# Laying out a whole kernel's instructions by due times, with shared buffers and PSUM banks

## The chip, the cores and the metric

One core of a Trainium2 chip runs the kernel. The metric is the device time of one execution in microseconds, as a median over runs. The kernel before takes 353.24 us (three runs, 352.86 to 353.85). Runs carry a state, fast or slow; unless said otherwise every number below comes from fast runs.

## The reference

A polysketch attention (4 batches, 4 heads, sequence 1088, head size 32, sketch size 8), whose output of 128 columns goes through a phase mixing over the tokens:

```python
def phi(x):
    a = np.einsum('rd,bhsd->bhsr', S1, x)
    b = np.einsum('rd,bhsd->bhsr', S2, x)
    return np.einsum('bhsi,bhsj->bhsij', a, b).reshape(*x.shape[:-1], r * r)
q_p, k_p = phi(q), phi(k)
kv  = np.einsum('bhsf,bhsd->bhfd', k_p, v)
num = np.einsum('bhsf,bhfd->bhsd', q_p, kv)
den = np.einsum('bhsf,bhf->bhs', q_p, np.sum(k_p, axis=2))[..., None] + 1e-06
x = num / den                                # (B, S, 128) after the heads are joined
theta = x @ w_theta
yr = np.einsum('ts,bsd->btd', w_tok_r, x * np.cos(theta))
yi = np.einsum('ts,bsd->btd', w_tok_i, x * np.sin(theta))
u = x + yr + yi
out = u + np.maximum(u @ w_ch, 0.0)
```

The two `w_tok` matrices (1088 x 1088) arrive as 64-bit floats and are turned into fp32 on the chip, in 34 pieces of 128 x 544. Each piece costs one load, three ScalarE instructions and two VectorE instructions (the tiles `st`, `step`, `wT`). PSUM is the memory into which TensorE puts its results, in eight banks that the kernel gives out. In names of tiles: `z` are the inputs of the mixing (they lie in two of the staging buffers, so the profile calls them `zst` before and `st` after the change), `lv` the feature levels of the queries, `fl`, `dn` and `rd` the denominators, `feat` the products of features, `uT` and `ot` the output, `cm` and `tl` small matrices made from the keys; `cut_r` and `cut_z` belong to many short steps that split small matrices into fp16 levels.

## The kernel before

It uses fixed pools and a fixed order of five priority levels, in which weight conversion goes along with batch 0's attention:

```python
ps_w = ctx.enter_context(tc.tile_pool(name="ps_w", bufs=3, space=PSUM))
ps_acc = ctx.enter_context(tc.tile_pool(name="ps_acc", bufs=2, space=PSUM))
ps_y = ctx.enter_context(tc.tile_pool(name="ps_y", bufs=3, space=PSUM))
# ... cut
levels = {nm: state.cur_priority + i * 100000
          for i, nm in enumerate(("first", "weights", "out", "attention", "mixing"))}
# ... cut
def load_f32(dst, src):               # one weight piece
    # ... cut
    st = stg.tile([P, PIECE], I64, tag="st", name="st")[:p, :n]
    nc.sync.dma_start(st, src)
    lo, hi = split(st)
    step = stg.tile([P, PIECE, 2], I16, tag="step", name="step", bufs=2)[:p, :n]
    x = dst.bitcast(I32)
    A.activation(dst, hi.bitcast(F32), AF.Copy, scale=2.0**-112)
    A.activation(step[:, :, 1].bitcast(F16), hi.bitcast(F32), AF.Copy, scale=2.0**-60)
    A.activation(step[:, :, 0], lo.bitcast(U32), AF.Copy, scale=2.0**-29)
    ts(x, x, 3, ALU.logical_shift_left)
    tt(V, x, x, step.rearrange("p n t -> p (n t)").bitcast(I32), ALU.add)
# ... cut
    matrices(0); keys_values(0, spare); attention(0)      # level "first"
with level("attention"):
    keys(1)
    attention(1)
    keys(2)
mixing(0, True)
with level("attention"):
    attention(2)
    keys(3)
mixing(1, False)
# ... batches 2 and 3 alike
```

Of the kernel before, what the change touches and what calls it, by code (L numbers as in the profile page):

```python
# [38 lines left out]
TINY = 2.0**-60  # L39
PIECE = 544  # L40


@with_exitstack
def kernel(
# [23 lines left out]
    const = ctx.enter_context(tc.tile_pool(name="const", bufs=1))  # L68
    stg = ctx.enter_context(tc.tile_pool(name="stg", bufs=4))
    ld = ctx.enter_context(tc.tile_pool(name="ld", bufs=1))  # L70
    work = ctx.enter_context(tc.tile_pool(name="work", bufs=2))
    sm = ctx.enter_context(tc.tile_pool(name="sm", bufs=2))
    xp = ctx.enter_context(tc.tile_pool(name="xp", bufs=2))
    ps_w = ctx.enter_context(tc.tile_pool(name="ps_w", bufs=3, space=PSUM))
    ps_acc = ctx.enter_context(tc.tile_pool(name="ps_acc", bufs=2, space=PSUM))
    ps_y = ctx.enter_context(tc.tile_pool(name="ps_y", bufs=3, space=PSUM))

    V, A = nc.vector, nc.scalar



    state = tc.trace_state
    levels = {nm: state.cur_priority + i * 100000
              for i, nm in enumerate(("first", "weights", "out", "attention", "mixing"))}

    @contextmanager
    def level(nm):
        kept, state.cur_priority = state.cur_priority, levels[nm]
        yield
        levels[nm], state.cur_priority = state.cur_priority, kept  # L90
# [10 lines left out]

    def psum(pool, tag, dt=F32, n=512):
        return pool.tile([P, n], dt, tag=tag, name=tag)
# [14 lines left out]
    def load_f32(dst, src):  # L118






        p, n = dst.shape
        if src.dtype == F32:
            nc.sync.dma_start(dst, src)
            return
        st = stg.tile([P, PIECE], I64, tag="st", name="st")[:p, :n]
        nc.sync.dma_start(st, src)  # L130
        lo, hi = split(st)
        step = stg.tile([P, PIECE, 2], I16, tag="step", name="step", bufs=2)[:p, :n]
        x = dst.bitcast(I32)
        A.activation(dst, hi.bitcast(F32), AF.Copy, scale=2.0**-112)  # L134
        A.activation(step[:, :, 1].bitcast(F16), hi.bitcast(F32), AF.Copy, scale=2.0**-60)  # L135
        A.activation(step[:, :, 0], lo.bitcast(U32), AF.Copy, scale=2.0**-29)  # L136
        ts(x, x, 3, ALU.logical_shift_left)
        tt(V, x, x, step.rearrange("p n t -> p (n t)").bitcast(I32), ALU.add)

    def load_pair(src, n, tag, copies=1):  # L140

        p = src.shape[0]
        m = p * copies
        hi = const.tile([P, n], F32, tag=f"{tag}_hi", name=f"{tag}_hi")[:m]
        lo = const.tile([P, n], F32, tag=f"{tag}_lo", name=f"{tag}_lo")[:m]
        if src.dtype == F32:
            for i in range(copies):
                nc.sync.dma_start(hi[i * p:(i + 1) * p], src)
            V.memset(lo, 0.0)
            return hi, lo  # L150
        st = const.tile([P, n], I64, tag=f"{tag}_st", name=f"{tag}_st")[:m]
        for i in range(copies):
            nc.scalar.dma_start(st[i * p:(i + 1) * p], src)
        wl, wh = split(st)
        x = magnitude(hi, wh)
        y = const.tile([P, n], I32, tag=f"{tag}_y", name=f"{tag}_y")[:m]
# [4 lines left out]
        z = const.tile([P, n], I32, tag=f"{tag}_z", name=f"{tag}_z")[:m]  # L161
# [6 lines left out]
    ident = const.tile([P, P], F32, tag="ident", name="ident")  # L168
    make_identity(nc, ident)
    ones = const.tile([P, P], F32, tag="ones", name="ones")  # L170
    V.memset(ones, 1.0)
    halfpi = const.tile([P, 1], F32, tag="halfpi", name="halfpi")
    V.memset(halfpi, math.pi / 2.0)

    hm = const.tile([P, H], F32, tag="hm", name="hm")
# [3 lines left out]
    hmT = const.tile([P, P], F32, tag="hmT", name="hmT")[:H]  # L179
    t_ = psum(ps_acc, "acc")  # L180
    nc.tensor.transpose(t_[:H, :P], hm, ident)
    A.activation(hmT, t_[:H, :P], AF.Copy, scale=512.0)

    bdm = const.tile([P, H, D], F32, tag="bdm", name="bdm")
    ts(bdm, hm.unsqueeze(2).to_broadcast([P, H, D]), 2.0**-15, ALU.mult)

    hmf = const.tile([P, 6, H], F32, tag="hmf", name="hmf")
# [9 lines left out]
    def powers(m, n, lhs=None, pool=(ps_acc, "acc")):  # L197


        t = psum(*pool)  # L200
        nc.tensor.transpose(t[:n, :P], m, ident)
        mx = sm.tile([P, 1], F32, tag="mx", name="mx")[:n]
# [4 lines left out]
        dg = sm.tile([P, H], F32, tag="dg", name="dg")[:n, :n]  # L207
        ts(dg, ident[:n, :n], mx, ALU.mult)
        o = psum(*pool)
        nc.tensor.matmul(o[:, :n], ones[:n, :], dg, start=True, stop=lhs is None, skip_group_check=True)  # L210
        w = n
        if lhs is not None:
            nc.tensor.matmul(o[:, w:w + 1], lhs, mx, start=False, stop=True, skip_group_check=True)
            w += 1
        s = sm.tile([P, H + 1], F32, tag="pw", name="pw")
# [3 lines left out]
    def cut4(dst, x0, rest, c0, c1, near=1, p=P):  # L219
# [3 lines left out]
        r = sm.tile([P, (B - 1) * P], F32, tag="cut_r", name="cut_r", bufs=1)[:p, :n]  # L223
        z = sm.tile([P, (B - 1) * P], F32, tag="cut_z", name="cut_z", bufs=1)[:p, :n]
# [19 lines left out]
    def spread(m, cs, z):  # L244

        o = m[:, :, cs].rearrange("p l (h r) -> p l h r", h=H)
        for o_, z_, f in ((o[:, 0:4], z, hmf[:, 0:4]), (o[:, 4:6], z[:, 0:2], hmf[:, 4:6])):
# [7 lines left out]
    def load(b, names):  # L255
        for nm in names:
            src = {"k": k, "q": q, "v": v}[nm]
            t = ld.tile([P, NC, H, D], F32, tag=f"ld_{nm}", name=f"ld_{nm}")
            nc.sync.dma_start(t.rearrange("p c h d -> p (c h d)"), src[b].rearrange("p c h d -> p (c h d)"))
            tiles[nm, b] = t  # L260

    ipk = const.tile([P, B, 2, H], F32, tag="ipk", name="ipk")
    gm = const.tile([P, 2, B, H], F32, tag="gm", name="gm")
    kvbd = []
    for b in range(B):
        t = const.tile([P, 2, 2 * D], F32, tag=f"kvbd{b}", name=f"kvbd{b}")
# [3 lines left out]
    w2 = const.tile([P, 2, DM], F32, tag="w2", name="w2")  # L270
    wT = const.tile([P, NK, S], F32, tag="wT", name="wT")


    def keys_slices(b):

        kn = tiles["k", b]
        m4 = sm.tile([P, H], F32, tag="m4", name="m4")
# [5 lines left out]
        kx = work.tile([P, NC, H, D], F32, tag="qx", name="kx", bufs=1)  # L283
# [3 lines left out]
        ks = work.tile([P, 3, NC * P], F16, tag="ksl", name="ksl", bufs=1)  # L287
# [7 lines left out]
    def keys_sums(b, cm, pool=(ps_acc, "acc")):  # L295
# [3 lines left out]
        gp = psum(*pool).rearrange("p (x n) -> p x n", x=4)  # L299

        for c in range(NC):
            cs = slice(c * P, (c + 1) * P)
            nc.tensor.matmul(gp[:, 0:3], ks[:, 1, cs], ks[:, 0:3, cs],
                             start=(c == 0), stop=False, skip_group_check=True)
            nc.tensor.matmul(gp[:, 0:4:3], ks[:, 2, cs], ks[:, 0:3:2, cs],
# [3 lines left out]
        t = psum(ps_acc, "acc")[:, :2 * P].rearrange("p (x n) -> p x n", x=2)  # L309
        for i in range(2):  # L310
            nc.tensor.transpose(t[:, i], cm[:, 2 * i], ident)
        tt(V, cm[:, 0:3:2], cm[:, 0:3:2], t, ALU.add)

    def keys_matrix(bs, cm):
# [3 lines left out]
        cz = work.tile([P, NL, nb, P], F16, tag="cz", name="cz", bufs=1)  # L318
# [3 lines left out]
        tp = psum(ps_acc, "acc")[:, :nb * NL * R].rearrange("p (b l r) -> p b l r", b=nb, l=NL)  # L322
        for i in range(nb):
            for l in range(NL):
                nc.tensor.matmul(tp[:, i, l:NL], cz[:, l, i], sz[:, 0:NL - l, 0:R],
                                 start=(i == 0 and l == 0), stop=(l == NL - 1), skip_group_check=True)
        n = nb * R
        tl = sm.tile([P, NL, nb, R], F32, tag="tl", name="tl", bufs=1)
        V.tensor_copy(tl.rearrange("p l b r -> p b l r"), tp)
        tl = tl.rearrange("p l b r -> p l (b r)")  # L330
        tz = sm.tile([P, NL, n], F16, tag="tz", name="tz", bufs=1)
# [406 lines left out]
```

## Time and profile before

| | before |
|---|---|
| span of the profiled run | 354.1 us |
| TensorE, VectorE, ScalarE busy | 271.9, 237.8, 167.0 us |
| first input of batch 0's mixing (z) | 117.45 us |
| TensorE idle (span less busy) | 82.2 us |

In the profile, PE is TensorE, PEld its weight loads, DVE VectorE, ACT ScalarE, POOL GpSimd and SP the load queue. One more view is needed for the comparison later: the windows of the profile, cut at 91, 120 and 165 us. The columns are window, length, busy time of PE, PEld, DVE, ACT and POOL with their instructions, granted clock, DMA share and GB/s.

```profile
0.00:91.00 91.00, 33.56 (x157) 24.63 (x157) 69.26 (x265) 70.93 (x124) 0.70 (x6) 0.76 0.68 229
91.00:120.00 29.00, 13.72 (x48) 10.20 (x49) 24.51 (x41) 19.46 (x34) 0.00 (x0) 0.50 0.20 69
120.00:165.00 45.00, 44.83 (x248) 31.60 (x247) 28.98 (x93) 17.05 (x39) 0.00 (x0) 0.97 0.13 40
165.00:350.00 185.00, 179.54 (x904) 124.83 (x902) 115.08 (x284) 59.06 (x136) 0.00 (x0) 0.98 0.07 22
```

At 165 us 179.8 us of TensorE's work is still to come (0.2 us of it after 350 us, where the window ends), and the span ends 9.3 us later than 165 + 179.8. A busy TensorE runs at nearly full clock there (0.98), so the time left is the work left. In the first 120 us TensorE was busy for 47.3 us, much of it at half clock.

### The profile page before, as it was taken

Reading aid. Unit: us, or ns where it says so; the run is one execution under the profiler, and the core shown is the slowest. Engines: PE = TensorE matmul, PEld = TensorE weight load, DVE = VectorE, ACT = ScalarE, POOL = GpSimd, SP = SyncE. Lnnn points to the kernel's source line nnn. Section 1 sums busy time; section 2 is a strip of 40 time slices with the busy share of each in tenths; the row PEclk is TensorE's granted clock in tenths of the full one; section 3 lists DMA queues with packets and bytes.
Section 4 is the critical chain, followed back from the end, with each engine's and each line's share of the span. In section 5 each row is a group of like instructions: output and inputs, shape, how many; then the busy total and the mean of one; then the engine's idle time right before and its main releaser. Section 6 shows DMA issues by size and latency. Waiting matters only on the chain.

```text
span 354.1 us, 4014 instructions
## 1 busy us (share of the span) xinstructions
PE 271.9 (77%) x1355; PEld 191.3 (54%) x1355; DVE 237.8 (67%) x681; ACT 167.0 (47%) x333; POOL 0.7 (0%) x6
## 2 busy tenths in 40 slices
PE   0406680127236799999978999999999999999994
PEld 0304480014125576675646778567776866776662
DVE  4897868884998178748986576887769289332111
ACT  0799839999955556043113365132456320442000
POOL 0000000000000000000000000000000000000000
PEclk9999955556555599999987999999999999999998
DMA  7668519884800004010010014000000000000000
GB/s 276 228 236 280 168 62 311 274 297 149 274 22 1 2 1 136 0 67 1 2 44 19 2 67 129 6 23 24 1 19 2 0 24 0 23 20 0 22 22 19
DMA packets 11604, 28.78 MB, mean 81 GB/s; under 512 B 1216, under 2 KB 5568, under 8 KB 11584
## 3 DMA queue, kind: packets, MB, share of 16 engines
q1 hardware_dynamic: 11376, 28.51, 24.1%
q8 instruction: 10, 0.16, 0.2%
q14 instruction: 10, 0.08, 0.1%
q10 hardware_dynamic: 208, 0.02, 0.0%
HBM read 26.30 MB, written 2.23 MB: 81 GB/s over the span
## 4 chain that ended last, share of the span: by engine, by line
PE 62%; DVE 17%; ACT 13%; DMA 4%; issue 1%; ACTq 0%; SPq 0%
PE y L560 31%; PE w L513 5%; ACT step L135 3%; PE acc L395 3%; ACT step L136 3%; PE w L533 3%; PE y L395 2%; PE w L507 2%; ACT lv L447 2%; PE y L570 2%; DVE wT L93 2%; PE w L385 2%; DMA s_t_st<-s_t 2%; ACT wT L134 2%; DVE kx L93 1%
## 5 line engine op out<-in xcount | busy, mean ns | idle before, releaser
L560 PE MATMUL y<-wT,zst 128*128 128x384 f32 (+1 forms) x384 | 134.9, 482 | 2.0 <-DVE zst L93 1.9
L560 PEld LDWEIGHTS y<-wT,zst 128*128 128x128 f32 x384 | 68.7, 193 | 32.2 <-DVE zst L93 3.2
L579 ACT COPY ot<-y 128x384 f32<-128x384 f32 (+2 forms) x16 | 5.9, 398 | 58.3 <-PE y L574 53.9
L135 ACT ACTIVATE step<-st 128x544 f16<-128x544 f32 (+1 forms) x35 | 27.8, 794 | 6.0 <-DVE wT L93 6.0
L513 PEld LDWEIGHTS w<-kvbd,qpT 128*128 128x128 f32 x144 | 22.0, 217 | 13.0 <-ACT qpT L511 11.0
L136 ACT ACTIVATE step<-st 128x544 int16<-128x544 uint32 (+1 forms) x35 | 27.5, 786 | 0.0
L93 DVE CUSTOM_DVE_ANT_0 wT<-wT,step 128x1088 uint16<-128x1088 uint16 x34 | 24.4, 718 | 4.5 <-ACT step L136 3.8
L513 PE MATMUL w<-kvbd,qpT 128*128 128x64 f32 x144 | 24.4, 305 | 3.8 <-ACT qpT L511 3.7
L134 ACT ACTIVATE wT<-st 128x544 f32<-128x544 f32 x34 | 23.2, 685 | 2.0 <-DMA st<-w_tok 1.9
L93 DVE TENSOR_TENSOR uT<-xT,y 128x384 f32<-128x384 f32 (+1 forms) x12 | 6.3, 528 | 22.5 <-PE y L560 22.5
L511 ACT COPY qpT<-w 128x256 f32<-128x256 f32 x36 | 12.7, 368 | 18.0 <-PE w L507 17.5
L507 PE MATMUL w<-ident,qp 128*128 128x128 f32 x72 | 14.0, 299 | 7.9 <-DVE qp L93 7.9
L530 ACT COPY xT<-w 128x384 f32<-128x384 f32 x12 | 5.7, 476 | 25.2 <-PE w L528 25.2
L100 DVE SCALAR_TENSOR_TENSOR tt<-tn,w 128x384 f32<-128x384 f32 x12 | 6.6, 552 | 14.9 <-ACT tn L537 14.9
L447 ACT COPY lv<-w 128x384 f32<-128x384 f32 x36 | 14.9, 499 | 2.9 <-PE w L446 2.9
L97 DVE TENSOR_SCALAR wT<-wT 128x544 int32<-128x544 int32 x34 | 14.6, 434 | 1.7 <-ACT wT L134 1.6
L507 PEld LDWEIGHTS w<-ident,qp 128*128 128x128 f32 x72 | 9.9, 168 | 8.9 <-ACT wT L134 7.9
L93 DVE TENSOR_TENSOR kp<-ks 128x768 f32<-128x768 f32 x12 | 11.4, 953 | 4.5 <-PE acc L395 2.5
L444 PE MATMUL w<-mv,q 128*128 128x384 f16 x36 | 13.2, 368 | 0.9 <-DVE mv L93 0.9
L395 PEld LDWEIGHTS acc<-ld_v,kp 128*128 128x128 f32 x108 | 13.1, 192 | 1.5
L93 DVE TENSOR_TENSOR zst<-x,tn 128x384 f32<-128x384 f32 (+1 forms) x12 | 6.1, 512 | 11.3 <-ACT tn L540 11.3
L533 PEld LDWEIGHTS w<-w,xT 128*128 128x128 f32 x72 | 10.7, 215 | 5.0 <-ACT xT L530 4.4
(228 smaller groups left out, 503.8 us busy)
## 6 DMA issues: line engine op xcount, KB each, us to landing
st<-w_tok SPq DMA_DIRECT2D x34, 544.0 KB, 4.6
ld_k<-k_l SPq DMA_DIRECT2D x4, 576.0 KB, 4.0
ld_q<-q_l SPq DMA_DIRECT2D x4, 576.0 KB, 4.3
ld_v<-v_l SPq DMA_DIRECT2D x4, 576.0 KB, 3.6
out<-ot SPq DMA_DIRECT2D x8, 192.0 KB, 2.1
out<-ot SPq DMA_DIRECT2D x4, 128.0 KB, 1.8
st<-w_sq SPq DMA_DIRECT2D x1, 256.0 KB, 4.5
out<-ot SPq DMA_DIRECT2D x4, 32.0 KB, 1.9
```

Source lines behind the costliest of these rows:

```text
L93: eng.tensor_tensor(out=o, in0=a, in1=b, op=op)
L97: V.tensor_scalar(out=o, in0=a, scalar1=s1, scalar2=s2, op0=op0, **kw)
L134: A.activation(dst, hi.bitcast(F32), AF.Copy, scale=2.0**-112)
L135: A.activation(step[:, :, 1].bitcast(F16), hi.bitcast(F32), AF.Copy, scale=2.0**-60)
L136: A.activation(step[:, :, 0], lo.bitcast(U32), AF.Copy, scale=2.0**-29)
L395: nc.tensor.matmul(kv[:, n], kp[:, i * H + 2 * n:i * H + 2 * n + 2].rearrange("p h i j -> p (h i j)"), vn[:, c, 2 * n:2 * n + 2].rearrange ...
L444: nc.tensor.matmul(lp, q0, flat[:, 0:4 * W], start=True, stop=False, skip_group_check=True)
L447: A.copy(lv[:, :, :, c].rearrange("p l t n -> p (l t) n"), lp.rearrange("p (x n) -> p x n", n=HR))
L507: nc.tensor.transpose(tr[:, n * P:(n + 1) * P], qp[:, i * H + 2 * n:i * H + 2 * n + 2].rearrange("p h i j -> p (h i j)"), ident)
L513: nc.tensor.matmul(num[:, i * P + n * 2 * D:i * P + (n + 1) * 2 * D], qpT[:, n], kvbd[b][:, n], start=True, stop=True)
L533: nc.tensor.matmul(th[:, i * P:(i + 1) * P], xT[:, i * P:(i + 1) * P], w2[:, 0], start=True, stop=True)
L560: nc.tensor.matmul(yp[:, :t1 - t0], z, wT[:, i, t0:t1], start=(i == 0), stop=(i == NK - 1))
```

## The change

Its intent is to remove the idle TensorE of the lead-in. No operation is issued while the program is written. Each is recorded with its reads, writes and a rough duration. The mixing matmuls get due times (90, 130, 170 and 210 us for the four batches), everything before them inherits an earlier due time through its dependencies, and a greedy simulation then picks, for each engine, the most urgent of what could start. Buffers and PSUM banks are given out in that simulated order, first come first served, all 8 banks being one set. The arithmetic stays. The diff, cut to its core:

```diff
+START = 90, 130, 170, 210
+BIG = 5
+PACE = 1.0
+class Order:
+    WAIT = 0.05
+    def duration(self, engine, call, out, ins):
+        ...
+        if engine == "ACT":
+            return 0.06 + n / 1100, 0.14
+    def dues(self):
+        for op in reversed(self.ops):
+            for n in op.behind:
+                other = self.ops[n]
+                other.due = min(other.due, op.due - op.cost - other.late)
+    def lay_out(self):
+        ...
+                    t, op = min(((t, o) for t, o in starts if t <= first + self.WAIT),
+                                key=lambda x: (x[1].due, x[1].n))
+        ...
+                cost *= 1.0 if use > 0.4 else 2.0
-    ps_w = ctx.enter_context(tc.tile_pool(name="ps_w", bufs=3, space=PSUM))
-    ps_acc = ctx.enter_context(tc.tile_pool(name="ps_acc", bufs=2, space=PSUM))
-    ps_y = ctx.enter_context(tc.tile_pool(name="ps_y", bufs=3, space=PSUM))
+    def psum():
+        return order.buffer(ps, "w", [P, 512], F32, 8)
     def mix_sums(b, gs, yps):
-                nc.tensor.matmul(yp[:, :t1 - t0], z, wT[:, i, t0:t1], start=(i == 0), stop=(i == NK - 1))
+                order.due = START[b] + (PACE * n if len(gs) > 1 else 0.65 * (g * NK + n))
+                T.matmul(yp[:, :t1 - t0], z, wT[:, i, t0:t1], start=(n == 0), stop=(n == NK - 1))
     def mix_out(b, g, yp):
+        order.due += 10
-    with level("first"):
-        load(0, "kqv")
+    load(0, "k")
+    ...  (both S matrices as one load)
+    for b in range(B):
+        ...
+        matrices(b)
+        keys_features(b)
+        query_slices(b)
+        keys_values(b)
+        features(b)
+        denominators(b, 0, NC)
+        for g in range(NG):
+            mixed(b, g, numerator(b, g))
+        if b == 0:
+            for i in rows:
+                for n in range(0, S, PIECE):
+                    load_f32(wT[:, i, n:n + PIECE], w_tok[i][:, n:n + PIECE])
+        mixing(b)
+    order.lay_out()
```

## The prediction

> **What bounds the kernel now.** I read the page's summary first, then the windows of each engine, then the timeline of the stretch in which TensorE is idle, then the chain that ended last.
>
> ```profile
> PE 271.9 (77%) x1355; PEld 191.3 (54%) x1355; DVE 237.8 (67%) x681; ACT 167.0 (47%) x333; POOL 0.7 (0%) x6
> ...
> PE   0406680127236799999978999999999999999994
> ...
> DVE  4897868884998178748986576887769289332111
> ACT  0799839999955556043113365132456320442000
> ...
> PEclk9999955556555599999987999999999999999998
> ```
>
> The kernel has two halves. Up to the fourteenth slice (about 118 us) TensorE is mostly idle and VectorE and ScalarE are full; from there TensorE is full to the end. The windows cut at 118 us, where the first mixing matmul starts, say it in numbers (columns: window, length, busy time of PE, PEld, DVE, ACT, POOL, granted clock, DMA share, GB/s):
>
> ```profile
> 0.00:118.00 118.00, 45.34 (x202) 33.66 (x202) 92.82 (x304) 89.51 (x156) 0.70 (x6) 0.70 0.57 193
> 118.00:350.00 232.00, 226.30 (x1153) 157.60 (x1153) 145.00 (x379) 76.99 (x176) 0.00 (x0) 0.98 0.08 25
> ...
> 180.00:200.00 20.00, 16.47 (x84) 12.11 (x83) 12.60 (x47) 7.76 (x20) 0.00 (x0) 0.83 0.09 28
> ```
>
> So the time is a lead-in of 118 us, a dense TensorE stretch of 232 us with one soft spot at 180 to 200 us, and 4 us of drain. The dense stretch is bound by TensorE: VectorE has 145 us of work in it, ScalarE 77. The question is what sets the 118.
>
> ```profile
> 57.45 0.18 DVE L329 COPY tl<-acc 128x32 f32<-128x32 f32 x1
> 57.55 0.43 DVE L97 TENSOR_SCALAR wT<-wT 128x544 int32<-128x544 int32 x1
> 57.90 0.17 DVE L97 TENSOR_SCALAR tz<-tl 128x8 f16<-128x8 f32 x1
> 57.98 1.34 DVE L192 TENSOR_REDUCE m<-ld_k 128x4 f32<-128x1152 f32 x1
> 59.24 0.16 DVE L93 TENSOR_TENSOR cut_r<-tl,tz 128x8 f32<-128x8 f32 x1
> 59.31 0.72 DVE L93 CUSTOM_DVE_ANT_0 wT<-wT,step 128x1088 uint16<-128x1088 uint16 x1
> 59.95 0.16 DVE L100 SCALAR_TENSOR_TENSOR cut_z<-tl,cut_r 128x8 f32<-128x8 f32 x1
> ```
>
> These lines are in time order. The 0.16 us steps (tl, tz, cut_r, cut_z) are batch 0's attention chain, on which everything later waits. Between each two of them stands a weight conversion (wT, 0.43 and 0.72 us) or even the first operation of batch 1 (m<-ld_k, 1.34 us). The waits show the price on TensorE, and the chain shows what a dense TensorE does:
>
> ```profile
> PE acc L335 <- DVE tz L97: 10.8, 2, 10.6
> ...
> 319.19 11.61 PE y L560 x36
> ...
> 340.71 7.01 PE y L560 x26
> ```
>
> The wait for tz is 10.6 us at one place. The last two lines (start, length, what) give dense mixing rates: 11.61/36 = 0.32 us a record at 384 columns, 7.01/26 = 0.27 at 320; an fp32 matmul is two records.
>
> **What the Trainium skill says.** "TensorE: Matmul & The Clock Gate", Part 1, says that the clock is half speed unless TensorE was busy for a window of about 3.4 us. The trace agrees: 0.50 in every window between 50 and 80 us and between 90 and 120 us, 1.00 from 130 to 180. In the first 40 us the profile says 1.00, but the fp16 pair of 384 and 256 columns there starts every 0.53 us, 1.2 columns per ns, against 768/0.32 = 2.4 in the dense end, so that reading is not to be believed. The same page ("Architectural detail") says that VectorE and ScalarE are strict FIFOs and only weight loads are pulled ahead on TensorE. So an instruction issued behind an unready one cannot pass it: order is all that the change changes. The trace has VectorE idle between 113.5 and 117.45 us for one tn while later work existed. "Perfetto Trace Analysis", "Identifying the Most-Contended Engine", warns that matmul busy time is no measure of headroom; hence I use start-to-start rates. "PSUM — Partial Sum Buffer", Specifications, gives 8 banks; the kernel splits them 3, 2 and 3, and the waits for a bank are small here (the kp and qpT rows, a few us).
>
> **The change, part by part.** Arithmetic is the same: same matmuls, same conversions. On VectorE one product per batch becomes two (four extra instructions, about 4 x 0.1 = 0.4 us), the two small S matrices are split as one (some 20 instructions of 0.1 us saved, 2 us), and six small mv copies fall to two (0.7 us). Together nothing that matters beside 237.8 us. What changes is order.
>
> TensorE's total at full clock. Mixing: 17 rows x (2 x 0.64 + 0.54) = 31 us a batch. Attention, a batch: numerators 36 records x 0.105 (eight in 0.84 in the chain) = 3.8; key values 36 x 0.107 = 3.9; phase product 18 x 0.143 = 2.6; key features 18 x 0.14 = 2.5; feature matmuls 9 x 864 columns / 2.4 = 3.2; key sums 9 x 640 / 2.4 = 2.4; 45 transposes x 0.11 = 5; some 25 small ones = 3.5: 27 us. Output, 3 us. Four batches: 4 x 61 = 244 us. Cross-check: what was left at 118 us took 232 us, of which the soft spot lost about 3.5 us idle and 3.4 us of clock, so 225; batch 0's attention without its last 8 us is the other 19. Sum 244 again.
>
> VectorE: about 9 us of set-up, 34 weight pieces x (0.36 + 0.66 start to start) = 35, and (237.8 - 44)/4 = 48 a batch, of which 3 in the output.
>
> (a) The lead-in. First z of batch 0 is at 117.45 us now. The S matrix is loaded right after k from one queue instead of behind k, q and v on another (first use at 8.0 us now, about 4.5 then): -3 us. The short-step chain from 57.5 to 79 us (22 us for some 35 steps of 0.1 and five TensorE hops of about 0.5, which need about 8): -13. Key slices to key sums (15.5 to 31 us, work of about 9): -6. Denominators (86.4 to 106.3 us, of which 19 wT operations and three qp): -5. Sum -27: first z at about 90 us. This is also the author's due time for batch 0's mixing, which I take as a sign and no proof. The weights must be there too: ScalarE needs 34 x 1.88 (start to start) = 64 plus some 25 for batch 0, VectorE 35 + 9 + 45 = 89, so both allow the last row at about 100, while mixing batch 0 runs from 90 to about 122 with its rows in order of arrival.
>
> (b) The rest. At 90 us TensorE will have done 19 us of batch 0 and about 4 of batch 1 (key transposes and features, which need only ScalarE). Left: 244 - 23 = 221. At 100% that ends at 311, and with the drain of 4 at 315. The 118 to 350 us stretch was dense at this very accounting (225 of 232), so I add no further loss, but neither a gain.
>
> (c) VectorE as co-bound. It must do 9 + 35 + 48 + 45 = 137 us before batch 1's last z, so not before about 142 at 96%. Until then TensorE has 27 + 31 + 27 + 5 = 90 us to do. Then 154 us are left for it: 296. That is the floor of this order, and it needs both engines without a gap. Thus 296 to 315; gaps from a fixed order whose durations are rough (VectorE records run 0.07 us over what the layout assumes) push up, an earlier first z down. I take 312.
>
> **The rivals.** (1) The early start is bought with a hole: mixing 0 ends at about 122, batch 1's z come at 135 to 142, and TensorE starves for 10 to 15 us in between and falls back to half clock. For it: 0.50 clock wherever TensorE was sparse before. Against: batch 1's early work can fill while weights are still arriving. Result 322 to 330. (2) A fixed order fits the chip badly: one misjudged duration makes a FIFO wait, and this repeats in each batch. For it: three FIFOs, about 4,000 instructions, no slack in the dense part. Against: the assumed durations match the trace (0.36 + 0.65 for a weight step, 0.11 for a transpose, 0.65 per mixing matmul), and the kernel before is also a fixed order. Result 335 to 360. (3) The layout packs better than I think: VectorE never idles in the lead-in, z at 80 and batch 1 far along. Result 290 to 300. (4) Loads: 26.3 MB at the 290 GB/s of the first window is 91 us, so the last weights land before they are needed, unless the six staging buffers, two of which hold z, delay them. Small, up to 5 us.
>
> **Range and chances.** Central 312 us, 0.88 of before. Rivals 1 and 3 are about a fifth each and give the ends of the range, 294 and 332. Rival 2 at its worst makes it the same or slower. Faster by over 2% (below 346): 0.93; same 0.05; slower 0.02.
>
> **What would show it right or wrong.** Right: first y<-wT matmul near 90 us (a); no wT conversion between the short cut_r and cut_z steps; from there TensorE in nines to the end, at clock 1.00; TensorE matmul count unchanged, VectorE busy within 3 us of 237.8. Step (b) is wrong if the dense stretch is much shorter than 221 us although it started at 90: then TensorE's work was done in the lead-in, or my sum is too large. Step (c) is wrong if there is a hole after mixing 0. All is wrong if the first mixing still starts after 110 us, or if waits of 2 us and more recur in each batch.

## More of the kernel before

While it is built, the changed kernel computes its own estimate of the end: 303.6 us. That number was not seen before the prediction; the experiments use such estimates.

## The result, and the profile after

The changed kernel takes 325.61 us (median of four runs, 322.53 to 328.55; the slowest of them is slow, and the median of the three fast ones is 323.99), and its results are correct. The ratio is 0.9194, with a 95% interval of 0.9105 to 0.9282. Ratios here are the mean time of one kernel's fast runs over that of the other's of the same rounds, so not quite the ratio of the medians quoted. Each experiment's ratio is to the kernel before, on its own chip.

The page of the changed kernel, profiled at 327.23 us:

```profile
PE 267.8 (82%) x1355; PEld 190.2 (58%) x1355; DVE 233.9 (72%) x663; ACT 167.1 (51%) x331; POOL 0.7 (0%) x6
...
PE   4569563519979998940999999988999999999993
...
DVE  5889997798879788799644982998688499441011
ACT  4564489993599999713153425225552412650001
...
PEclk9859655556979999985589999999999999999999
```

TensorE is in nines from the thirteenth slice (about 98 us) where it had been from the fifteenth. Then it falls to 4 and 0 in two slices (138 to 155 us), with 5 in the clock row from 146 to 163 us, and is dense afterwards. ScalarE's row is full at 49 to 73 us and again from 90 to 130. The same windows as before:

```profile
0.00:91.00 91.00, 56.81 (x321) 44.33 (x321) 76.98 (x258) 61.44 (x117) 0.70 (x6) 0.70 0.51 187
91.00:120.00 29.00, 27.37 (x94) 16.66 (x95) 25.12 (x69) 28.52 (x49) 0.00 (x0) 0.94 0.56 188
120.00:165.00 45.00, 30.19 (x157) 22.13 (x156) 36.95 (x83) 23.12 (x46) 0.00 (x0) 0.77 0.28 97
165.00:350.00 185.00, 153.38 (x787) 107.03 (x785) 94.86 (x255) 54.01 (x121) 0.00 (x0) 0.99 0.04 11
```

At 165 us 153.4 us of TensorE's work is left, against 179.8 before. That is 26.4 of the 28.7 us by which the span got shorter. The rest, time idle after 165 us, is 7.0 against 9.3. So nearly the whole gain is work that TensorE has done sooner. The third line shows what was not gained: of 45 us TensorE was busy for 30.19, at clock 0.77.

Where the lead-in got shorter shows on VectorE's timeline of batch 0 (start, length, instruction). Before:

```profile
37.03 0.69 DVE L93 TENSOR_TENSOR cm<-y,bdm 128x512 f32<-128x512 f32 x1 [1.66 <-PE y L305]
...
78.15 0.16 DVE L97 TENSOR_SCALAR nz<-cut_z 128x8 f16<-128x8 f32 x1
...
86.37 1.05 DVE L100 SCALAR_TENSOR_TENSOR fl<-lv 128x864 f32<-128x864 f32 x1
...
105.88 0.18 DVE L93 TENSOR_TENSOR rd<-rd,gm 128x36 f32<-128x36 f32 x1
```

After, with the first mixing input as the last line (all carry L305, the line that issues the recorded operations):

```profile
24.45 0.69 DVE L305 TENSOR_TENSOR cm<-w,bdm 128x512 f32<-128x512 f32 x1 [1.36 <-PE w L305]
...
32.42 0.17 DVE L305 COPY tl<-w 128x32 f32<-128x32 f32 x1
...
45.91 0.16 DVE L305 SCALAR_TENSOR_TENSOR cut_z<-nl,cut_r 128x8 f32<-128x8 f32 x1
45.99 0.72 DVE L305 CUSTOM_DVE_ANT_0 wT<-wT,step 128x1088 uint16<-128x1088 uint16 x1
...
51.43 0.16 DVE L305 TENSOR_SCALAR nz<-cut_z 128x8 f16<-128x8 f32 x1
...
64.16 1.06 DVE L305 SCALAR_TENSOR_TENSOR fl<-lv 128x864 f32<-128x864 f32 x1
...
83.94 0.20 DVE L305 TENSOR_TENSOR rd<-rd,gm 128x36 f32<-128x36 f32 x1
```

```profile
91.90 0.56 DVE L305 TENSOR_TENSOR st<-x,tn 128x384 f32<-128x384 f32 x1 [1.68 <-ACT tn L305]
```

The key sums are read into `cm` at 24.5 instead of 37.0 us, `tl` follows at 32.4 instead of 57.5 (the prediction shows that line), the last short step is at 51.4 instead of 78.2, the denominators start at 64.2 instead of 86.4 and end at 84.1 instead of 106.1, and the first z comes at 91.90 instead of 117.45. So 25 of the 25.6 us are won by `tl`: before it no weight conversion stands in VectorE's queue any more (the first is at 36.52). The line at 45.99 is one of eight weight conversions that still stand between the short steps from 45.91 to 51.43; the stretch from the first `nz` step to the last takes 5.9 us, as before (5.8).

The hole, on TensorE's timeline (idle time and its releaser in brackets) and on VectorE's:

```profile
142.38 0.55 PE L305 MATMUL w<-ident,big 128*128 128x128 f32 x3 [0.57 <-ACT fT L305]
154.63 1.65 PE L305 MATMUL w<-uT,w 128*128 128x384 f32 x2 [11.71 <-DVE uT L305]
156.07 0.64 PE L305 MATMUL w<-ident,feat 128*128 128x128 f32 x2
```

```profile
140.68 0.58 DVE L305 TENSOR_SCALAR big<-lv,dgr 128x576 f32<-128x576 f32 x1
...
142.51 0.95 DVE L305 TENSOR_TENSOR feat<-fl 128x768 f32<-128x768 f32 x1
...
146.79 2.00 DVE L305 TENSOR_REDUCE dn<-lv 128x36 f32<-128x288 f32 x2
...
153.16 0.95 DVE L305 TENSOR_TENSOR feat<-fl 128x768 f32<-128x768 f32 x1
154.03 0.55 DVE L305 TENSOR_TENSOR uT<-xT,w 128x384 f32<-128x384 f32 x1
```

TensorE stands for 11.71 us because the next matmul in its queue needs `uT`, an output step of batch 0, which VectorE's queue has behind all of batch 1's denominators (136 to 153 us) and about 4 us of batch 2's key slices (`ksl`, `big`) between them. The first of batch 1's three feature products (`feat<-fl`) is made at 142.51, but its transposes stand behind that matmul in TensorE's queue (156.07); the other two come only after the denominators, at 153.16 and 160.41.

### The profile page after: what moved, and what is told of

It reads as the page before. It is cut to its first block, busy times and chain, and to the rows that moved or that the text cites. A ratio compares the mean times of both kernels' runs of the same rounds, so it can differ in the third digit from the quotient of the medians.

```text
span 325.4 us, 4041 instructions
## 1 busy us (share of the span) xinstructions
PE 267.8 (82%) x1355; PEld 190.2 (58%) x1355; DVE 233.9 (72%) x663; ACT 167.1 (51%) x331; POOL 0.7 (0%) x6
## 4 chain that ended last, share of the span: by engine, by line
PE 53%; ACT 22%; DVE 16%; DMA 4%; issue 3%; SPq 1%; ACTq 0%
PE w L305 53%; ACT step L305 11%; ACT wT L305 4%; DVE lv L305 3%; DVE big L305 3%; ACT lv L305 2%; DMA st<-w_tok 2%; DVE feat L305 1%; DVE dn L305 1%; DVE ksl L305 1%; ACT tn L305 1%; DMA big<-k_l 1%; DMA big<-q_l 1%; DVE fl L305 1%; ACT big L305 1%
## 5 line engine op out<-in xcount | busy, mean ns | idle before, releaser
L305 PE MATMUL w<-wT,st 128*128 128x384 f32 (+1 forms) x384 | 134.9, 481 | 2.3 <-DVE st L305 2.2
L305 PEld LDWEIGHTS w<-wT,st 128*128 128x128 f32 x384 | 68.0, 193 | 33.4 <-DVE st L305 3.1
L305 ACT ACTIVATE step<-st 128x544 f16<-128x544 f32 (+2 forms) x70 | 52.2, 813 | 0.0
L305 ACT COPY fT<-w 128x256 f32<-128x256 f32 (+1 forms) x48 | 18.6, 401 | 31.7 <-PE w L305 31.5
L305 PEld LDWEIGHTS w<-kvbd,fT 128*128 128x128 f32 x144 | 23.9, 216 | 6.4 <-ACT fT L305 3.6
L305 DVE CUSTOM_DVE_ANT_0 wT<-wT,step 128x1088 uint16<-128x1088 uint16 x34 | 24.1, 718 | 3.2 <-ACT step L305 3.2
L305 PE MATMUL w<-kvbd,fT 128*128 128x64 f32 x144 | 24.9, 285 | 1.4 <-ACT fT L305 1.2
L305 PE MATMUL w<-ident,feat 128*128 128x128 f32 x72 | 17.3, 307 | 10.6 <-DVE feat L305 9.6
L305 PE MATMUL w<-mv,qsl 128*128 128x384 f16 (+2 forms) x108 | 19.1, 323 | 7.8 <-DVE mv L305 5.8
L305 ACT ACTIVATE wT<-st 128x544 f32<-128x544 f32 x34 | 23.4, 714 | 0.5 <-DMA st<-w_tok 0.5
L305 PEld LDWEIGHTS w<-big,feat 128*128 128x128 f32 x144 | 20.8, 202 | 4.6 <-DVE feat L305 0.9
L305 ACT COPY ot<-w 128x384 f32<-128x384 f32 (+2 forms) x16 | 5.9, 398 | 33.3 <-PE w L305 33.3
L305 ACT COPY lv<-w 128x384 f32<-128x384 f32 x36 | 15.8, 498 | 13.1 <-PE w L305 13.1
L305 PE MATMUL w<-big,feat 128*128 128x64 f32 x144 | 21.7, 280 | 0.8 <-DVE feat L305 0.8
L305 PE MATMUL w<-uT,w 128*128 128x384 f32 (+1 forms) x24 | 11.0, 545 | 12.3 <-DVE uT L305 12.3
L305 PEld LDWEIGHTS <-qsl 128*128 128x128 f16 x108 | 11.4, 109 | 15.6 <-issue 10.4
L305 PEld LDWEIGHTS w<-ident,feat 128*128 128x128 f32 x72 | 11.5, 177 | 13.6 <-issue 10.9
L305 PE MATMUL w<-ident,big 128*128 128x128 f32 x72 | 14.2, 343 | 5.3 <-DMA big<-k_l 3.6
L305 DVE TENSOR_SCALAR wT<-wT 128x544 int32<-128x544 int32 x34 | 14.6, 437 | 5.6 <-ACT wT L305 5.5
L305 PE MATMUL w<-ksl 128*128 128x384 f16 x72 | 17.5, 376 | 0.0
L305 DVE TENSOR_TENSOR uT<-xT,w 128x384 f32<-128x384 f32 (+1 forms) x12 | 6.3, 529 | 14.7 <-PE w L305 14.7
L305 DVE SCALAR_TENSOR_TENSOR uT<-w,uT 128x384 f32<-128x384 f32 (+1 forms) x12 | 6.4, 532 | 14.4 <-PE w L305 14.4
```

The costliest lines, as they stand in the source:

```text
L305: op.call(*r, **{k: x.real() if isinstance(x, View) else x for k, x in op.kw.items()})
```

## The experiments

All were run for three timed rounds beside the kernel before, whose median was 353.63, 353.79, 354.11 and 353.95 us in the four jobs. Theory A blamed the hole on VectorE's load, B on the order of the output in the queues, C on ScalarE's queue.

### e1: the weight conversion's VectorE work laid out but not issued

```diff
+        k = len(order.ops)
         ts(x, x, 3, ALU.logical_shift_left)
         tt(V, x, x, step.rearrange("p n t -> p (n t)").bitcast(I32), ALU.add)
+        for op in order.ops[k:]:
+            op.unsent = dst.buf.tag == "wT"
@@ lay_out, where the operations are issued
         for op in out:
+            if getattr(op, "unsent", False):
+                continue
```

> The changed kernel in exactly its own order, but the 68 VectorE instructions that finish the mixing weights (a shift and an add for each of 34 pieces, about 35 us of VectorE) are laid out and then not issued; the result is wrong on purpose. Theory A (the hole at 140 to 160 us is VectorE not having produced batch 1's z, because the conversions share it in the lead-in): the hole shrinks to under 5 us, the first mixing matmul comes at 85 us or earlier, and the time falls to 300 to 308 us. Theory B (the hole is made by the fixed order: the batch 0 output stands at the head of TensorE's queue behind a late VectorE instruction): that order is unchanged, so the hole stays near 15 us and the time is 318 us or more.

Measured: 324.88 us (323.31 to 327.67), ratio 0.9185, wrong results (relative error 0.687). VectorE was busy for 203.1 us instead of 233.9 and the end did not move. The first z came at 89.36 and batch 1's at 163.97 instead of 169.35; from 140 to 160 us TensorE had 8.47 us of work. Theory A falls: taking 31 us off VectorE is worth nothing in this order.

### e2: the output of batch 0 due early

```diff
-        order.due += 10
+        order.due += -15 if b == 0 else 10
```

> The changed kernel with one number of its due times changed: the output of batch 0 (uT and what follows) is due before its mixing instead of 10, 20 and 30 us after it, so it is laid out as soon as it can run and no longer behind batch 1's denominators. The layout's own plan ends at 298.0 instead of 303.6 us, with batch 1's first z 6 us earlier. Theory A (VectorE starved of time): the same VectorE work has to be done before batch 1's z, so the hole only shifts; 322 to 327 us. Theory B (queue order makes the hole): the wait of 11.7 us for uT goes and the time falls by 6 to 12 us, to 313 to 319. If the plan is a good guide to the chip (it ran 20 us short on the changed kernel), 318.

Measured: 328.28 us (326.43 to 329.67), ratio 0.9270. The hole is filled, as this window shows:

```profile
140.00:160.00 20.00, 17.69 (x91) 13.38 (x90) 18.83 (x39) 5.67 (x15) 0.00 (x0) 0.88 0.03 10
```

But the first z moved from 91.90 to 105.69 us, and batch 1's came at 166.27. Theory B expected 313 to 319; it falls as an explanation of the time, for the idle time went elsewhere. But the one number changed the whole layout, the lead-in too, so this run doesn't show what closing the hole alone would be worth.

### e3: the banks divided 3, 2 and 3 again

```diff
-    def psum():
-        return order.buffer(ps, "w", [P, 512], F32, 8)
+    def psum(tag="w"):
+        return order.buffer(ps, tag, [P, 512], F32, {"w": 3, "acc": 2, "y": 3}[tag])
```

with the tags "acc" and "y" given to the calls that used those pools before.

> The changed kernel with its 8 PSUM banks split again as in the kernel before, 3 for general work, 2 for sums and powers, 3 for the mixing; due times and everything else stay. My prediction gave sharing little: by that the time is 322 to 330 us. Rival: sharing carries a good part of the gain, because mixing groups and attention groups take turns: 335 to 345. The layout's own plan says 318.6 against 303.6 us, so with the 20 us by which it runs short about 338.

Measured: 336.25 us (335.73 to 339.92), ratio 0.9532. The window after 165 us:

```profile
165.00:350.00 185.00, 158.87 (x829) 111.74 (x829) 99.62 (x262) 58.59 (x129) 0.00 (x0) 0.97 0.05 16
```

TensorE had done 48.69 us by 91 us instead of 56.81, and 158.87 instead of 153.38 was left at 165. So with the layout, sharing the banks is worth 11 to 12 of the 28 us (against all runs of the change, or its fast ones).

### e4: the weight conversion first

```diff
+            order.due = 0.0
             for i in rows:
                 for n in range(0, S, PIECE):
                     load_f32(wT[:, i, n:n + PIECE], w_tok[i][:, n:n + PIECE])
+            order.due = math.inf
```

> The changed kernel with the weight conversions given due time 0, so that they go ahead of batch 0's attention chain on VectorE and ScalarE as they did in the kernel before; nothing else changes. My step (a) says that the gain is this order: the first mixing matmul moves back to 115 to 125 us and the time to 345 to 358, so the gain is gone. Rival: the gain comes from denser packing later on, and the order of the lead-in matters less: under 338 us. The layout's own plan says 336.5 with mixing from 110 us, so with its 20 us about 356.

Measured: 357.29 us (355.73 to 358.18), ratio 1.0087. The first z came at 119.70 us, about where it was before the change. TensorE had 14.50 us of work in the 29 us from 91 to 120, and 176.7 us is left at 165 (1.3 of it after 350 us, where this window ends):

```profile
165.00:350.00 185.00, 175.36 (x896) 124.72 (x895) 120.45 (x305) 61.94 (x141) 0.00 (x0) 0.94 0.06 18
```

Shared banks, layout and due times for all the rest are in this kernel, and it is no faster than the kernel before. Without the new order of the weight conversion against the chain nothing of the gain is left. It isn't quite the old order, for due time 0 puts the conversions ahead of all other work: the last short step comes at 71.1 us, the denominators at 92.8.

### e5: two of the three ScalarE instructions of the conversion left out as well

```diff
+        k = len(order.ops)
         A.activation(step[:, :, 1].bitcast(F16), hi.bitcast(F32), AF.Copy, scale=2.0**-60)
         A.activation(step[:, :, 0], lo.bitcast(U32), AF.Copy, scale=2.0**-29)
         ts(x, x, 3, ALU.logical_shift_left)
         tt(V, x, x, step.rearrange("p n t -> p (n t)").bitcast(I32), ALU.add)
+        for op in order.ops[k:]:
+            op.unsent = dst.buf.tag == "wT"
```

> The changed kernel's order, unchanged, but the weight conversion's VectorE instructions (68, as in e1) and its two ScalarE step instructions per piece (68, about 46 us) are laid out and not issued, so the results are wrong on purpose; one ScalarE copy per piece stays, so that the loads still have a reader. Theory C (ScalarE's queue between 45 and 135 us, with the conversions ahead of batch 1's own work, is what holds batch 1 back): ScalarE falls to about 120 us, the last level copy of batch 1 comes about 25 us earlier (near 105 instead of 136), the hole at 140 to 160 us closes, the first z of batch 1 comes near 140 to 145 instead of 169, and the end at 296 to 304. If the hole is made by something other than the conversions (the half clock alone, or TensorE's own order), z of batch 1 stays after 160 and the time above 318. In between says a part.

Measured: 310.23 us (308.57 to 311.44), ratio 0.8756, wrong results. ScalarE falls from 167.1 to 124.4 us, the first z comes at 80.62 and batch 1's at 153.59, 16 us sooner. The hole is still there, only earlier:

```profile
139.41 1.65 PE L307 MATMUL w<-uT,w 128*128 128x384 f32 x2 [11.39 <-DVE uT L307]
```

The result lies between my two cases: z of batch 1 came sooner, but the hole didn't close. Against e1, whose VectorE is as empty, taking 43 us off ScalarE is worth 0.043 in the ratio, 15 us: ScalarE's queue does set how soon everything comes. It does not make the hole. The same matmul waits for the same `uT` for 11.39 us, so the hole belongs to the order itself. The changed kernel's ScalarE timeline shows how the queue holds the chain up (two of the nine level copies, and the conversion between them):

```profile
55.53 0.48 ACT L305 COPY lv<-w 128x384 f32<-128x384 f32 x1
55.88 0.85 ACT L305 ACTIVATE step<-st 128x544 f16<-128x544 f32 x1
56.55 0.49 ACT L305 COPY lv<-w 128x384 f32<-128x384 f32 x1
```

The levels `lv` of batch 0, for which the denominators wait, leave ScalarE one conversion apart. In e5, from the last short step to the first denominator (`fl`) takes 7.4 us instead of 12.7.

### e6: the kernel before with one pool of 8 banks

```diff
-    ps_w = ctx.enter_context(tc.tile_pool(name="ps_w", bufs=3, space=PSUM))
-    ps_acc = ctx.enter_context(tc.tile_pool(name="ps_acc", bufs=2, space=PSUM))
-    ps_y = ctx.enter_context(tc.tile_pool(name="ps_y", bufs=3, space=PSUM))
+    ps_w = ps_acc = ps_y = ctx.enter_context(tc.tile_pool(name="ps", bufs=8, space=PSUM))
-        return pool.tile([P, n], dt, tag=tag, name=tag)
+        return pool.tile([P, n], dt, tag="b", name=tag)
```

> The kernel before with one single pool of 8 PSUM banks in place of pools of 3, 2 and 3, its own instruction order and scheduling kept: the sharing of banks by itself. If sharing is worth something by itself, 335 to 345 us. If sharing only pays together with the new order (which is what I expect, since the first z of batch 0 in the kernel before waits for the weights and not for a bank), 349 to 356.

Measured: 525.51 us (524.42 to 528.06), ratio 1.4847, correct. Neither case of mine was near. Two of its waits (who waits for what; us in total, times, the longest):

```profile
ACT ot L577 <- PE y L572: 114.6, 10, 25.2
DVE uT L91 <- PE y L558: 95.8, 10, 18.4
```

VectorE and ScalarE wait for TensorE everywhere: for its mixing sums (`y`) 18 and 25 us at a time, where the longest such wait of ScalarE in the changed kernel is 15.0 us. TensorE is busy for 350.6 us, at a mean clock of 0.699. So sharing was of no use to the old order, and harmful. I take the reason to be that a single rotating pool hands banks out in the order in which they were asked for, so that the next use stands behind long sums; no run isolates that.

### e7: one conversion step on GpSimd

```diff
-        A.activation(step[:, :, 1].bitcast(F16), hi.bitcast(F32), AF.Copy, scale=2.0**-60)
+        G.tensor_scalar(out=step[:, :, 1].bitcast(F16), in0=hi.bitcast(F32), scalar1=2.0**-60, scalar2=None, op0=ALU.mult)
```

and an engine "POOL" in the layout, with a rough duration of 0.1 + n/550 us, 1.09 us for 544 columns.

> The changed kernel with one of the two ScalarE step instructions of each weight piece done by the idle GpSimd (34 instructions, about 23 us off ScalarE), laid out with that engine added. Correct results. The layout's own estimate ends at 305.7 in place of 303.6, so plan plus the 20 us of drift seen so far gives 326. If ScalarE in the lead-in is what costs (theory C), the drift is smaller, first z of batch 1 near 155 to 160, and 312 to 320. If GpSimd is slow at it or gets in VectorE's way, the lead-in gets longer: 330 to 345.

Measured: 337.83 us (336.95 to 339.31), ratio 0.9546, correct. Groups of instructions by form (busy us, mean ns, idle before), first of e7, then of the changed kernel:

```profile
L308 POOL TENSOR_SCALAR step<-st 128x544 f16<-128x544 f32 x34 | 67.2, 1975 | 45.5 <-DVE mxn L308 24.3 <-DVE wT L308 13.2 <-DVE cut_z L308 4.0
...
L308 ACT ACTIVATE step<-st 128x544 int16<-128x544 uint32 x34 | 27.3, 820 | 2.9 <-DVE wT L308 2.8
...
L308 DVE TENSOR_SCALAR wT<-wT 128x544 int32<-128x544 int32 x34 | 21.3, 641 | 0.0
```

```profile
L305 DVE TENSOR_SCALAR wT<-wT 128x544 int32<-128x544 int32 x34 | 14.6, 437 | 5.6 <-ACT wT L305 5.5
```

GpSimd took 1.98 us for one instruction, against 0.82 us for ScalarE's and 1.09 in my estimate, and VectorE's shift of the weights, which e7 does not touch, went from 437 to 641 ns. VectorE as a whole rose from 233.9 to 248.5 us. The Trainium skill, "Perfetto Trace Analysis", Optimizing Scalar/DVE Operations, says that GpSimd and VectorE share an SBUF read port, which some VectorE operations hold exclusively, so that offloading between the two might not help. This trace agrees in that both engines got slower; it doesn't show the port itself.

### e8: durations corrected from the trace, constants searched again

```diff
-START = 90, 130, 170, 210
-BIG = 5
-PACE = 1.0
+START = 80, 120, 155, 190
+BIG = 4
+PACE = 1.83
-    WAIT = 0.05
+    WAIT = 0.03
+            if mybir.dt.size(out.dtype) == 2 and n == PIECE:
+                return 0.06 + n / 880, 0.14
             return 0.06 + n / 1100, 0.14
-                cost *= 1.0 if use > 0.4 else 2.0
+                cost *= 1.0 if use > 0.6 else 2.0
-        step = buf("step", [P, NC * P], I16, 3)...        # and "half", the same tag
+        step = buf("step", [P, NC * P], I16, 5)...
-        order.due += 10
+        order.due += 0
```

`use` is the layout's own guess of when TensorE's clock rises; no run here measures that point.

> The changed kernel laid out again with two rough durations corrected from the trace of the changed kernel (ScalarE's weight pieces 0.68 us in place of 0.55; the full TensorE clock from 60% recent use in place of 40%), and the layout's own constants searched under those durations: 5 step buffers and 4 big ones in place of 3 and 5, due-time spacing 40, 35, 35, no lateness for the output chains, pace 1.83. The estimate under these durations is 296.3, against 307.6 for the constants of the change: 11 us less. If the estimates' differences carry over, 314 us; if they are noise at this size, as e2 showed, anything from 315 to 330. I expect 318.

Measured: 313.28 us (312.84 to 314.02), ratio 0.8847 (0.8795 to 0.8899), correct. This beats both kernels: 40 us less than before on the same chip, and 12 less than the change's median, taken on another. Its windows from 120 us on:

```profile
120.00:165.00 45.00, 40.01 (x238) 31.01 (x237) 38.90 (x85) 27.50 (x58) 0.00 (x0) 0.89 0.23 74
165.00:350.00 185.00, 140.92 (x691) 96.34 (x690) 88.16 (x246) 45.47 (x105) 0.00 (x0) 0.99 0.04 11
```

The first z (87.98) and batch 1's (166.30) come only 3 to 4 us sooner than in the change. But from 120 to 165 us TensorE is busy for 40.01 us in place of 30.19, and 140.92 in place of 153.38 is left at 165: 12.5 us, and the spans differ by 14.5.

### e9: no due times

```diff
-        self.cost, self.late, self.due = cost, late, due
+        self.cost, self.late, self.due = cost, late, math.inf
```

> The changed kernel's layout with every due time infinite: among the operations that could start, the one recorded first goes first; banks, buffers and rough durations as in the change. The layout's own estimate is 358.4 against 303.6. If the due times carry the gain (as e4 says of the lead-in alone), the estimate plus the 20 us seen so far: 372 to 384, slower than the kernel before. If recording and laying out by rough durations with shared banks is by itself most of the gain, 330 to 345.

Measured: three fast runs of 399.33, 398.71 and 393.77 us, ratio 1.1228 (1.1121 to 1.1335), correct. The profiled run was slow, 518.34 us at a mean clock of 0.54, so its trace is not used for times. Neither case of mine was right: 399 is 15 us above the worse one.

Recording and laying out alone, with shared banks, makes the kernel 12% slower than before. The due times carry more than the whole gain.

### e10: e8's constants without its corrected durations

The edit is e8's without the lines in `duration` and `use > 0.6`.

> e8's constants (buffers 5 and 4, due-time spacing 40, 35, 35, no lateness of the output chains, pace 1.83, window 0.03) with the change's own, uncorrected durations. Estimate 293.6 under those durations. If the constants are what made e8 faster, and the correction of durations does little, 308 to 318. If an order laid out by wrong durations misfits the chip as the change's did (plus 22), 313 to 318; if the correction of durations was the main thing, 320 to 328.

Measured: 314.57 us (313.04 to 315.36), ratio 0.8886 (0.8820 to 0.8952), correct. Nearly all of e8's gain is in the constants. VectorE's timeline at the place of the former hole:

```profile
145.52 0.95 DVE L305 TENSOR_TENSOR feat<-fl 128x768 f32<-128x768 f32 x1
...
146.88 0.95 DVE L305 TENSOR_TENSOR feat<-fl 128x768 f32<-128x768 f32 x1
...
150.35 0.96 DVE L305 TENSOR_TENSOR feat<-fl 128x768 f32<-128x768 f32 x1
```

The three feature products of batch 1, on which TensorE works next, come between the denominator steps at 145 to 151 us. In the change they come at 142, 153 and 160. VectorE had done the outputs of batch 0 by 140. The hole is filled in e8 too, where no idle time of TensorE from 118 to 172 us is longer than 0.99 us.

### e11: the corrected durations alone

The edit is e8's lines in `duration` and `use > 0.6`, nothing else.

> The change's own constants with e8's two corrected durations. Estimate 307.6 (under corrected durations). If a better fit of the durations is what made e8 faster, the end comes within 15 us of the estimate, as e8's did (296.3 against 313): 318 to 322 or less. If the constants made it, 323 to 330, no better than the change.

Measured: 324.79 us (323.37 to 325.18), ratio 0.9172, correct. The estimate for this kernel is 4 us above the change's, and so nearer to the chip, but no time is gained.

### e12: the buffer counts alone

The edit is e8's lines for `BIG` and `step`, nothing else.

> The change with two numbers changed: 5 buffers for the small step and half tiles in place of 3, and 4 of the big ones in place of 5 (so that it still fits), every due time and duration as in the change. It splits the gain of e10 (11 us): its estimate is 300.4 against 303.6. If the buffers made it, batch 2's key work fills the hole before 160 us and the time is 312 to 317; if the due times made it, the hole stays and the time is 321 to 328.

Measured: 324.88 us (324.02 to 325.44), ratio 0.9175, correct. I had tied 321 to 328 us to a hole that stays. The time is as said for that case, but the hole did not stay, it moved:

```profile
140.00:160.00 20.00, 19.06 (x148) 16.22 (x149) 15.87 (x62) 11.63 (x34) 0.00 (x0) 1.00 0.11 31
160.00:170.00 10.00, 3.15 (x20) 2.61 (x19) 10.00 (x16) 2.58 (x5) 0.00 (x0) 0.65 0.15 56
```

From 140 to 160 us TensorE is nearly full, then it stands in the next 10 us, and z of batch 1 is at 178.64 us. So the buffers alone bring nothing. The other constants are needed (spacing, lateness, pace and window); which of these four, and whether they would do without the buffers, was not separated.

### All runs together

| kernel | estimate of its layout | time, us | first z of batch 0 | TensorE work left at 165 us | span |
|---|---|---|---|---|---|
| before | none | 353.24 | 117.5 | 179.8 | 354.1 |
| after | 303.6 | 325.61 | 91.9 | 153.4 | 325.4 |
| e2 output early | 298.0 | 328.28 | 105.7 | 151.0 | 324.6 |
| e3 banks divided | 318.6 | 336.25 | 91.6 | 158.9 | 334.0 |
| e4 weights first | 336.5 | 357.29 | 119.7 | 176.7 | 356.1 |
| e7 GpSimd | 305.7 | 337.83 | 95.2 | 158.5 | 335.8 |
| e8 refit | 296.3 | 313.28 | 88.0 | 140.9 | 310.9 |
| e9 no due times | 358.4 | 399.02 | not used | not used | not used |
| e10 constants | 293.6 | 314.57 | 90.2 | 140.3 | 312.5 |
| e11 durations | 307.6 | 324.79 | 95.4 | 150.4 | 321.6 |
| e12 buffers | 300.4 | 324.88 | 98.3 | 147.9 | 323.5 |

(e9's median is over all four runs.) The span less 165 less the work left is between 5.0 and 8.6 us for the change, e2, e8, e10 and e11, and 9.3 to 14.4 for the others. The estimates are 17 to 25 us too low but for e2, e7 and e9 (30, 32, 41). They rank most of the big differences rightly, but put e7, whose duration on GpSimd was wrong, 13 us below e3, and it ran 2 us longer. Small differences they don't rank: e2 was to gain 6 us and lost 3.

Other parts of the change were not separated: the earlier load of the S matrices and the mixing rows in a new sequence.

## Why the prediction was right, and where its sum was off

Faster (0.93) and the range hold; 325.61 lies within 294 to 332, but 13.6 us above the 312 (323.99, the fast runs' median, 12.0 above). The central case, steps (b) and (c), did not come; a rival that I gave a fifth did, and it is the rivals that make the range wide enough. Step by step:

**(a) The lead-in, first z at about 90 us: right, its parts less so.** Measured 91.90. The parts, by the lines above:

| part of the lead-in | saving predicted, us | measured, us |
|---|---|---|
| up to the key sums (`cm`) | 9 | 12.6 |
| from `cm` to `tl` | not in the sum | 12.5 |
| short steps, `tl` to the last `nz` | 13 | 1.7 |
| features, last `nz` to `fl` | not in the sum | -4.5 |
| denominators, `fl` to `rd` | 5 | -0.3 |
| from `rd` to z | not in the sum | 3.6 |
| sum | 27 | 25.6 |

So the total was right partly by luck. The mechanism, conversions in the chain's way, was right, but it acted before `tl` and hardly in the stretch that I had blamed. From `cm` to `tl`, in the steps on 128 x 128 matrices, ten weight operations had stood in VectorE's queue, and batch 0's query slices and key products (`kp`) with them. The S matrix's first use came at 5.44 (8.02 before) instead of about 4.5. The features grew from 8.2 to 12.7 us, because the level copies stand between conversions on ScalarE (e5). In the denominators I had counted 19 weight operations; the trace has 12. After the change it has 5 there, but other work and waits took their place. That this order is needed is shown by e4, which puts the conversions first and is back at 357. My test "no wT conversion between the short steps" failed: eight stand there. So did the narrower one on VectorE's busy time, 233.9 us against "within 3 us of 237.8"; the count of TensorE instructions, 1355, is the same.

**The weights by 100 us, mixing 0 from 90 to 122: wrong.** The last conversion ended at 135 us. I compared ScalarE's total (89 us) with the clock and took it as gapless. It was busy for 61.4 of the first 91 us, then full to 130, and mixing 0 went on to 136.5. e5 sizes it: 43 us less ScalarE work is 15 us less time.

**(b) The rest, 221 us of work and no loss but 4 us of drain: two errors.** From 91 us the windows give 27.37 + 30.19 + 153.38 = 210.9 us of work, 10 less than I had, and 234.4 - 210.9 = 23.5 us idle instead of 4. Of these, 14.8 are in the stretch from 120 to 165 us. The failed sentence is "I add no further loss".

**(c) VectorE could reach batch 1's last z by 142 us at 96%, and no hole after mixing 0: failed,** by the sign that I had named. VectorE's work was as I had summed it: 139.05 us by 165 us, against 137. But it took 165 us for it, 84%, and that last z started at 185.96. Its queue waited for other engines. More of VectorE's time was not what was missing either (e1).

**Rival 1 (the hole, 322 to 330) is what happened.** I gave it a fifth. It has the hole, the half clock (0.61 from 140 to 160 us) and the time. My reason for it, starvation between the end of mixing 0 and batch 1's z, was right; what makes it is the order, not a shortage: e8 and e10 do the same work with the hole filled, at 313 and 315, close to the 312 of the prediction. **Rival 2 (misfit in each batch)** is refuted: from 165 us TensorE is dense, with no listed wait of TensorE over 1.1 us. **Rival 3** did not come. **Rival 4 (loads):** the load queue issued nothing between about 13 and 39.7 us, and one weight load of 5.91 us stands in the chain that ended last; but ScalarE's idle time for weight loads is 0.5 us in all. The cost was not isolated.

**"The waits for a bank are small": right for the kernel before, wrong as a measure of what sharing gives.** e3 shows 11 to 12 us. Small waits in an old order do not tell what a new order needs. And e6 shows that one rotating pool under the old order costs 172 us.

**Small slips in the prediction:** its own items for the short steps (35 x 0.1 + 5 x 0.5) make 6 us and not 8. VectorE's idle time for `tn` starts at 114.17 us and not at 113.5. The rate of 768/0.32 takes two passes for each record as given; the plain comparison holds without it: the same pair of fp16 matmuls starts every 0.53 us at 31 us and every 0.27 us at 123.5 us.

## What to carry to other kernels

When the queues run in issue order, ask at each engine which queued instruction releases the bottleneck soonest; due times that spread backwards through the dependencies answer that, while laying out without them was 12% slower than the order by hand. Take a scheduler's estimate as good for differences of some 10 us here as long as its durations are measured (e7's was not), tune its constants by it, and let the chip decide. A filled hole is not yet a gain: in e2 and e12 the lead-in got longer or the hole moved. Count the bottleneck's work left at a fixed time; in every kernel of the table whose trace was used its difference from the kernel before agrees with that of the span to within about 5 us.

## What the Trainium skill lacked or had wrong

- "TensorE: Matmul & The Clock Gate", Part 1, warns that clock-gate events in a trace have been seen to be unreliable. The runs agree: before the change the granted clock reads 1.00 in the first 40 us, although the fp16 matmuls there start at half the dense rate (a pair of 384 and 256 columns every 0.53 us, and every 0.27 us at 123.5 us). The page does not say that this falls on the start of a kernel.
- That page gives the slow clock of an idle TensorE and a limit that takes several busy cores. In e9 a program on a single core ran once in 518.34 us at a mean clock of 0.54, and three times in 394 to 399 us at 0.78 to 0.81. Nothing that I read on the page explains it; the nearest is its note of a gate stuck at a quarter of the clock, where this trace reads 0.50 to 0.59 in every stretch of 50 us.
- "Perfetto Trace Analysis", Optimizing Scalar/DVE Operations, says that offloading to GpSimd might not help, and that section gives no size. In e7 the 128 x 544 scaling took 1.98 us there and VectorE's 128 x 544 shift slowed from 437 to 641 ns.
- "PSUM — Partial Sum Buffer", Specifications, gives the eight banks and not what dividing them costs. Here it was 11 to 12 us with the new order (e3), and sharing them in one pool in the old order cost 172 us (e6).
